# Linear attention and four-expert mixture: another opening, with other load queues, own buffers for each head pair and seven PSUM banks in the first layer

## The chip, the core and the metric

The kernel runs on one core of a Trainium2 chip. Its engines each take their instructions in order: PE multiplies matrices (its results go to PSUM, eight banks of 128 x 512 float32), DVE and ACT work element by element, POOL and SP here do little but issue DMA transfers. The metric is the device time of one execution in microseconds (us), less being better. Times in the profile count from the start of its span.

## The reference, cut to what matters

```python
q_p, k_p = phi(q), phi(k)             # phi(x) = where(x > 0, x, exp(x) - 1) + 1
kv  = einsum('bhsd,bhse->bhde', k_p, v)
z   = sum(k_p, axis=2)
num = einsum('bhsd,bhde->bhse', q_p, kv)
den = einsum('bhsd,bhd->bhs', q_p, z)[..., None] + 1e-06
x   = (num / den) as [4608, 512]      # 8 batches, 8 heads, 576 rows, 64 columns
p   = domain_probs / (domain_probs.sum(-1) + 1e-09)
for e in range(4):
    h = maximum(x @ w1[e], 0)         # w1[e]: 512 x 1024
    out += p[:, e:e+1] * (h @ w2[e])  # w2[e]: 1024 x 512
```

All inputs are float32; the kernel computes in float16 with float32 sums.

## The kernel before

The 576 rows of a batch are 512 rows, four of them on each of 128 partitions, and 64 rest rows. The 8 heads are taken as four pairs (`pr` 0 to 3). For each batch and pair, `attention` (L434) does: exp on ACT and two DVE operations for phi of k and of q (L456, L457), transposes of phi(q) (L484) and a copy to `qT` (L497), the sum kv with its column of ones for z (L515 to L523), a copy to `kvz` (L534), the numerator and denominator (L548, L550), and a division on DVE (L555, L556).

The mixture takes 512 rows at a time. Rows of batch 0 go through it in the plain way, an expert at a time: `first_l1` (L705) multiplies by w1 in chunks of 128 input columns (`dc`, four of them) and 128 hidden columns (`fj`, eight of them) and applies ReLU; `first_l2` (L744) multiplies by w2. All later rows go through units (`l1_seven`, `ssums`, `l2_unit`), which do each product in seven block products in place of eight, with sums of weight blocks that `sums_w1` and `sums_w2` prepare on DVE. Between the opening and the units, the attention of batch 1 runs among the mixture of experts 1 to 3 on batch 0.

The order is not that of the code. Every piece of work is handed to a `Plan` (L21) with an engine, an estimated duration, a priority and the keys that it reads and writes. The plan lays all pieces out in time, works deadlines back from PE, lays them out again, and the instructions are then written in that order, engine by engine. DMA pieces of POOL keep the order of the code. `T0` and `TU` (L163) are the planned start and pitch of the units. On the chip only the order and the waits on data count, not the planned times; the waits follow whole tiles, so that two users of different columns of one PSUM bank wait for each other.

Around the change:

- Loads (L293, L312): batch 0's pair 0 and its k and v rest rows are five DMAs in SP's queue; pairs 1 to 3 follow in POOL's, held until k of pair 0 has landed, and behind them the weights: w1 and w2 of expert 0, the q rest rows, expert 1, then batch 1's loads and experts 2 and 3. POOL has eight DMAs in flight at most. Weights and some of v turn to float16 on the way in.
- Buffers of batch 0's attention: three staging buffers for k, q and v, two `ek` and two `kqp`, used in turn; one PSUM bank each for transposes of phi(q) (`l2b[1]`), for the numerators (`at`) and for transposes of x (`tbank`, which is `l2b[3]`); kv and denominators share `l2b[2]`.
- Rest rows of k and v lie on 64 partitions (`kqr`, `vr`), a row of each head in a piece of 256 bytes.
- `turn_x` (L666) transposes the normalized rows of a pair into `xt0`, the right operand of the first layer; chunk `dc` of the first layer needs pair `dc`.
- `first_l1` for expert 0 runs four hidden chunks at once over `dc`, in four PSUM banks (`l1b` and `l2b[0]`), and the other four after them, three banks in turn. All ReLUs are ACT's (L713).
- `keep_warm` (L1073) fills planned gaps of PE up to 22 us (`WARM`) with matmuls whose result nobody reads.

Of the kernel before, what the change touches and what calls it, by code (L numbers as in the profile page):

```python
# [20 lines left out]
class Plan:  # L21
# [13 lines left out]
    def __init__(self):  # L35
        self.ops = []
        self.wr = {}
        self.rd = {}

    def add(self, eng, dur, pri, fn, r=(), w=(), move=0.0, after=0.0, lead=1.2):  # L40
        n = len(self.ops)
        deps = set()
        for key in r:
            if key in self.wr:
                deps.add(self.wr[key])
            self.rd.setdefault(key, []).append(n)
        for key in w:
            if key in self.wr:
                deps.add(self.wr[key])
            deps.update(x for x in self.rd.get(key, ()) if x != n)  # L50
        for key in w:
            self.wr[key] = n
            self.rd[key] = []
        self.ops.append(
            dict(eng=eng, dur=dur, pri=pri, fn=fn, deps=deps, move=move, after=after, lead=lead, w=w)
        )
        return n

    def deadlines(self):
# [10 lines left out]
        for n, o in enumerate(ops):  # L70
            if o["eng"] != "PE" and o["pri"] >= -99:
# [62 lines left out]
def kernel(  # L134
# [27 lines left out]
    WARM, COLD = 22.0, 28  # L162
    T0, TU = 79.0, 6.4  # L163
# [7 lines left out]
    def sb(name, shape, dt):  # L171
# [47 lines left out]
    v00 = vss[1].rearrange("p h c d -> p (h c d)").bitcast(FP16)[:, 2 * C * D :].rearrange(  # L219
        "p (h c d) -> p h c d", h=2, c=C  # L220
    )
    ones = sb("ones", [P, 2, 1], FP16)
    rc4 = sb("rc4", [P, 2 * C], FP32)
# [20 lines left out]
    def lk(i):  # L244

        return ("l2b2k", "l2b2n") if i == 2 else ("l2b%d" % i,)

    def stage_keys(i):

        if i < 2:  # L250
            return ("st", i, 0), ("st", i, 1), ("st", i, 2)
        return ("xp", 0), ("xp", 1), ("u2", 0)
# [35 lines left out]
    def v16(i):  # L288

        flat = vss[i].rearrange("p h c d -> p (h c d)").bitcast(FP16)  # L290
        return flat[:, 0 : 2 * C * D].rearrange("p (h c d) -> p h c d", h=2, c=C)

    def load_pair(b, pr, queue, pri, after=0.0, hold=None):  # L293
        hs = slice(2 * pr, 2 * pr + 2)
        n = 3 if b < 2 else 2
        i = rot("stage%d" % n, n) if n == 2 else rot("stage3", 3)
        stage[b, pr] = i
        kk = stage_keys(i)
        vo = vss[i] if b or queue == "SP" else v16(i)
        parts = [(k, kqs[i][:, 0], kk[0]), (v, vo, kk[2]), (q, kqs[i][:, 1], kk[1])]  # L300
        if b == 0:
            parts[1:] = parts[:0:-1]
        for t, o, key in parts:
            if (b, pr, key) == (0, 0, kk[1]):
                load_rest(0, "SP", 0, parts=(0,))
            keys = (key, "v00") if (b, key) == (1, ("st", 1, 2)) else (key,)
            dma(queue, pri, o, t[b, hs, 0:NT].rearrange("h (p c) d -> p h c d", c=C), keys,
                0.7,
                hold="w" if b == 2 else hold if key == kk[0] else None,
                mark="k0" if (b, pr, key) == (0, 0, kk[0]) else None, after=after)  # L310

    def load_rest(b, queue, pri, after=0.0, parts=(0, 1, 2)):  # L312
        par = b % 2
        rs = slice(par * R, par * R + R)
        for i in parts:
            t, o = ((k, kqr[rs, 0]), (v, vr[rs]), (q, kqr[rs, 1]))[i]
            dma(queue, pri, o, t[b, :, NT:S].rearrange("h s d -> s h d"), (("str", par, i),),
                1.1,
                hold="w" if b in (2, 3) else None, after=after)
# [26 lines left out]
    def probs(b0, b1, raw, keys, out_key, pri):  # L346
# [7 lines left out]
            r=keys, w=(out_key,))  # L354
# [10 lines left out]
    def rest_maps(b, pe_mode, pri, parts=(0, 1)):  # L365
# [19 lines left out]
        if not pe_mode:  # L385
            pl.add("SP", 1.25, pri + 1, lambda: nc.sync.dma_start_transpose(
                out=qTr[par][:, :, rs], in_=kqpr[rs, 1].rearrange("p h d -> p (h d)")),
                r=("qpr",), w=[("qTr", par, i) for i in range(DC)], move=0.9, lead=0.2)

# [44 lines left out]
    def attention(b, pr, pe_mode, pri, step, two=False):  # L434
# [16 lines left out]
        zi = pr if two else rot("kvz", 2)  # L451
# [8 lines left out]
        if two:  # L460
            vh = v00 if pr == 0 else v16(si)
            vk = "v00" if pr == 0 else sk[2]

        def vcast():
            if two:
                nc.scalar.copy(vh, vs)
            else:
                nc.scalar.copy(vp[:, :, :, 0:D].rearrange("p c h d -> p h c d"), vs)

        order_ = (0, 1)  # L470
        for i in order_:
# [4 lines left out]
            if i == 0 and not (two and pr):  # L476
                pl.add("ACT", 0.52, pri + step, vcast, r=(sk[2],), w=(vk,))
        if pe_mode:

            tq, tk = (l2b[1].bitcast(FP16), "l2b1") if two else (tbank, "l2b3")  # L480

            def turn():
# [4 lines left out]
                if two:  # L487
                    return
# [7 lines left out]
                   r=(("kqp", pi, 1), "ident") + (() if two else ("qpr",)), w=(tk,))  # L496
            pl.add("ACT", 0.5, pri + 3.5 * step, lambda: nc.scalar.copy(  # L497
                qT.rearrange("p c t -> p (c t)"), tq[:, 0:NT]), r=(tk,), w=(("qT", ti),))
            if not two:
                pl.add("DVE", 0.2, pri + 3.5 * step, lambda: nc.vector.tensor_copy(  # L500
                    qTr[par][:, pr, rs], tq[:, NT : NT + R]), r=(tk,), w=(("qTr", par, pr),))
# [6 lines left out]
        if two:  # L508
            kvs_, kvk = l2b[2][:, 0 : 2 * DE], ("l2b2k",)
        kv3 = kvs_.rearrange("p (h e) -> p h e", h=2)  # L510

        def kv():
            for c in range(C):
                if two:
                    nc.tensor.matmul(out=kv3[:, :, 0:D], lhsT=kp[:, c], rhs=vh[:, :, c],  # L515
                                     start=(c == 0), stop=False, skip_group_check=True)
                    nc.tensor.matmul(out=kv3[:, :, D:DE], lhsT=kp[:, c], rhs=ones,
                                     start=False, stop=False, skip_group_check=True)
                else:
                    nc.tensor.matmul(  # L520
                        out=kvs_, lhsT=kp[:, c], rhs=vp[:, c], start=(c == 0), stop=False
                    )
# [6 lines left out]
                skip_group_check=two,  # L529
# [7 lines left out]
        pl.add("PE", 0.42 if two else 0.3, pri + 4 * step, kv,  # L537
# [4 lines left out]

        if two:
            den = l2b[2][:, 256 : 256 + 2 * C].rearrange("p (c h) -> p c h", h=2)

            def nd0():
                for c in range(C):
                    nc.tensor.matmul(out=at[:, c * P : (c + 1) * P], lhsT=qT[:, c],  # L548
                                     rhs=kvz[:, :, 0:D], start=True, stop=True)
                    nc.tensor.matmul(out=den[:, c], lhsT=qT[:, c],  # L550
                                     rhs=kvz[:, :, D:DE], start=True, stop=True)

            def norm0():
                rc = rc4.rearrange("p (c h) -> p c h", h=2)
                nc.vector.reciprocal(rc, den)  # L555
                nc.vector.tensor_tensor(  # L556
                    out=xs[:, :, fs].rearrange("p c (h d) -> p c h d", h=2),
                    in0=at.rearrange("p (c h d) -> p c h d", c=C, h=2),
                    in1=rc[:, :, :, None].broadcast_to([P, C, 2, D]),
                    op=AO.mult,  # L560
                )

            pl.add("PE", 0.36, pri + 5 * step, nd0, r=(("qT", ti), ("kvz", zi)),
                   w=("at", "l2b2n"))
            pl.add("DVE", 0.83, pri + 5.5 * step, norm0, r=("at", "l2b2n"),
                   w=[("x", par, pr, c) for c in range(C)])
            return
# [77 lines left out]
    def sums_w2(e, pri):  # L645
# [11 lines left out]
        for o, a, b_, r, w in (  # L657
# [5 lines left out]
            pl.add("DVE", 0.62, pri, two(o, a, b_), r=r, w=w)  # L663


    def turn_x(pr, pri):  # L666
        fs = slice(pr * P, (pr + 1) * P)

        def go():
            for c in range(C):  # L670
                nc.tensor.transpose(
                    out=tbank[:, c * P : (c + 1) * P], in_=x_b[0][:, c, fs], identity=identh
                )

        pl.add("PE", 0.25, pri, go, r=[("x", 0, pr, c) for c in range(C)] + ["ident"], w=("l2b3",))
        pl.add("ACT", 0.5, pri + 0.5, lambda: nc.scalar.copy(xt0[:, pr, :], tbank[:, 0:NT]),
               r=("l2b3",), w=(("s4", 1, pr),))

    def mm1(e, fj, bank, dcs):
        for dc in dcs:  # L680
            nc.tensor.matmul(  # L681
                out=bank,
                lhsT=w1_sb[e][:, dc, fj * P : (fj + 1) * P],
                rhs=xt0[:, dc, :],
                start=(dc == 0),
                stop=(dc == DC - 1),
# [18 lines left out]
    def first_l1(e, pri, step, nb):  # L705
        ht = []
        banks = [(l1b[i], "l1b%d" % i) for i in range(3)]
        if nb == 4:
            banks += [(l2b[0], "l2b0")]
        ht = [rot("ht", len(hts)) for _ in range(FC)]  # L710

        def relu(fj, bank, key, pr_):
            pl.add("ACT", 0.5, pr_, lambda: nc.scalar.activation(hts[ht[fj]], bank, AF.Relu),  # L713
# [3 lines left out]
        if nb:  # L717
            b0 = cnt.get("l1", 0) if nb < 4 else 0
            for dc in range(DC):
                for fj in range(nb):  # L720
                    bank, key = banks[(b0 + fj) % nb]
                    p_ = pri + (dc * 4 + fj) * step
                    pl.add("PE", 0.216, p_,
                           lambda fj=fj, bank=bank, dc=dc: mm1(e, fj, bank, (dc,)),
                           r=w1k(e, dc, fj) + (("s4", 1, dc),), w=(key,))
                    if dc == DC - 1:
                        relu(fj, bank, key, p_ + 0.2)
            done = nb
            if nb == 4:
# [282 lines left out]
    load_pair(0, 0, "SP", 0)  # L1012
    load_rest(0, "SP", 0, parts=(1,))
    load_pair(0, 1, "POOL", 0, hold="k0")
    load_pair(0, 2, "POOL", 0)
    rest_maps(0, True, 3, (0,))
    for pr in range(DC):
        if pr == 3:
            load_pair(0, 3, "POOL", 0)
            load_w1(0, range(DC))  # L1020
            probs(0, 2, p5_b, ("p5",), "pnat0", 24)
            load_w2(0)
            load_rest(0, "POOL", 0, parts=(2,))
        attention(0, pr, True, 2.5 + pr, 0.4, two=True)
# [113 lines left out]
```

## Time and profile before

| | us |
|---|---|
| median of 7 runs | 498.86 |
| lowest and highest of the 7 | 497.93, 499.63 |
| profiled execution | 499.56 |
| span of its profile | 497.8 |
| PE busy in the span | 486.4 |
| DVE busy | 408.7 |
| ACT busy | 367.0 |

The span runs from the first to the last instruction of the program; the execution has 1.8 us more around it. Busy time of PE counts its filler matmuls too, and its ends are modelled, so it says where PE has instructions rather than how well it is used. In timelines a row is the start, the duration, the engine, the line, the operation and its tiles, how often it came in a row, and in brackets how long the engine had stood idle before it and what ended that. The name `w` covers w1 and w2, `s` covers the identity and some hidden tiles, `xp`, `u` and `vs` the staging buffers.

### The profile page before, as it was taken

How to read it: one execution, taken by the hardware profiler on the slowest of the kernel's cores; microseconds unless marked ns; L12 is line 12 of the kernel's file. 1: busy time of each engine (PE TensorE's matmuls, PEld its weight loads, DVE VectorE, ACT ScalarE, POOL GpSimd, SP SyncE). 2: the span in 40 equal slices, each digit the busy share in tenths (PEclk: the TensorE clock that was granted, in tenths of full speed). 3: DMA queues.
4: the chain of work that ended last, by engine and by line, in shares of the span. 5: the costliest groups of instructions: out<-in, count | busy, mean ns of one | idle time of the engine just before them, and what ended most of it. 6: DMA issues, size and time to landing. Idle time of an engine off the chain costs nothing.

```text
span 497.8 us, 15010 instructions
## 1 busy us (share of the span) xinstructions
PE 486.4 (98%) x6109; PEld 431.0 (87%) x6109; DVE 408.7 (82%) x1033; ACT 367.0 (74%) x690; POOL 41.7 (8%) x67
## 2 busy tenths in 40 slices
PE   7899999999999999999999999999999999999995
PEld 6544456999999999999999999999999999999995
DVE  5677999988998999899988899889988675767664
ACT  6635759988987798769876988689766767676641
POOL 7655710000000000000000000000000000000000
PEclk9999999999999999999999999999999999999999
DMA  8999988846674774765756765755623333523221
GB/s 227 197 235 196 262 169 187 222 103 175 126 161 121 167 170 133 128 167 118 171 126 158 148 150 119 169 139 123 161 54 85 36 97 43 77 55 86 45 44 42
DMA packets 125573, 67.11 MB, mean 135 GB/s; under 512 B 95520, under 2 KB 119600, under 8 KB 125504
## 3 DMA queue, kind: packets, MB, share of 16 engines
q1 hardware_dynamic: 116112, 51.79, 47.4%
q0 software_dynamic: 9232, 14.10, 14.0%
q8 instruction: 47, 0.77, 0.7%
q10 hardware_dynamic: 160, 0.26, 0.1%
q14 instruction: 22, 0.18, 0.1%
HBM read 45.16 MB, written 9.44 MB: 110 GB/s over the span
## 4 chain that ended last, share of the span: by engine, by line
PE 87%; DMA 7%; ACT 2%; DVE 1%; POOL 1%; issue 0%; DVEq 0%; POOLq 0%
PE l1b L835 40%; PE l2b L911 38%; DMA w<-in_moe_w_dram 4%; PE l2b L691 4%; PE l1b L681 3%; DMA kqr<-in_k_dram 2%; PE at L571 2%; DMA kq<-in_k_dram 2%; PE at L520 1%; ACT xp L795 0%; DVE ot L975 0%; POOL w L262 0%; ACT h L849 0%; ACT ek L379 0%; PE at L523 0%
## 5 line engine op out<-in xcount | busy, mean ns | idle before, releaser
L835 PEld LDWEIGHTS <-w 128*128 128x128 f16 x2048 | 133.4, 98 | 5.2
L849 ACT ACTIVATE h<-l1b 128x512 f16<-128x512 f32 x128 | 76.8, 600 | 53.6 <-PE l1b L835 48.4
L911 PE MATMUL l2b<-w,h 128*128 128x256 f16 x768 | 114.9, 273 | 0.0
L911 PE MATMUL l2b<-t,s 128*128 128x256 f16 x768 | 114.3, 273 | 0.0
L835 PEld LDWEIGHTS <-w1x 128*128 128x128 f16 x1536 | 100.1, 98 | 3.9 <-issue 0.2
L911 PEld LDWEIGHTS <-s 128*128 128x128 f16 x1024 | 90.9, 98 | 6.6
L855 DVE CUSTOM_DVE_ANT_0 h<-l1b,p 128x512 f16<-128x512 f32 x64 | 44.1, 690 | 46.0 <-PE l1b L835 42.7
L795 ACT ACTIVATE xp<-x,p_nat 128x512 f16<-128x512 f16 x112 | 77.5, 720 | 1.0 <-DVE x L584 0.5
L835 PE MATMUL l1b<-xT,w 128*128 128x128 f16 x1024 | 78.1, 219 | 0.0
L835 PE MATMUL l1b<-xs,w 128*128 128x128 f16 x1024 | 78.0, 219 | 0.0
L835 PE MATMUL l1b<-xs,w1x 128*128 128x128 f16 x1024 | 77.9, 219 | 0.1
L911 PEld LDWEIGHTS <-h 128*128 128x128 f16 x768 | 67.4, 98 | 4.5
L897 DVE TENSOR_TENSOR s<-h 128x512 f16<-128x512 f16 x128 | 53.9, 421 | 2.1
L852 ACT COPY l1b<-l1b 128x512 f32<-128x512 f32 x64 | 36.7, 574 | 12.2 <-PE l1b L835 11.5
L852 ACT COPY u<-l1b 128x512 f32<-128x512 f32 x64 | 37.5, 585 | 11.1 <-PE l1b L835 10.9
L855 DVE CUSTOM_DVE_ANT_0 h<-l1b,u 128x512 f16<-128x512 f32 x64 | 43.8, 685 | 1.1 <-PE l1b L835 0.4
L852 ACT COPY p<-l1b 128x512 f32<-128x512 f32 x64 | 37.4, 584 | 8.9 <-PE l1b L835 7.2
L472 ACT ACTIVATE ek<-kq 128x512 f16<-128x512 f32 x60 | 37.9, 632 | 4.8 <-DMA kq<-in_k_dram 3.9
L813 DVE TENSOR_TENSOR xs<-xT,xs 128x256 f16<-128x256 f16 x128 | 36.8, 288 | 3.4
L835 PE MATMUL l1b<-xT,w1x 128*128 128x128 f16 x512 | 39.0, 219 | 0.0
L911 PE MATMUL l2b<-w,s 128*128 128x256 f16 x256 | 38.4, 273 | 0.0
L457 DVE TENSOR_TENSOR kqp<-ek,kqp 128x512 f16<-128x512 f16 x64 | 27.2, 425 | 6.0 <-ACT ek L472 1.4
(128 smaller groups left out, 579.4 us busy)
## 6 DMA issues: line engine op xcount, KB each, us to landing
w<-in_moe_w_dram POOLq DMA_DIRECT2D x32, 256.0 KB, 8.3
out_dram<-ot SPq DMA_DIRECT2D x16, 512.0 KB, 3.6
kq<-in_k_dram SPq DMA_DIRECT2D x25, 256.0 KB, 3.2
kq<-in_q_dram SPq DMA_DIRECT2D x25, 256.0 KB, 3.6
vs<-in_v_dram SPq DMA_DIRECT2D x25, 256.0 KB, 3.7
kq<-in_k_dram POOLq DMA_DIRECT2D x5, 256.0 KB, 7.1
kq<-in_q_dram POOLq DMA_DIRECT2D x5, 256.0 KB, 6.1
xT<-xp SPq DMA_TRANSPOSE x64, 3.1
```

The costliest lines, as they stand in the source:

```text
L457: nc.vector.tensor_tensor(out=o, in0=ek[:, i], in1=o, op=AO.min)
L472: pl.add("ACT", 0.55, pri + i * step, lambda i=i: nc.scalar.activation(ek[:, i], kq[:, i], AF.Exp), r=(sk[i],), w=(("ek", ei, i),))
L681: nc.tensor.matmul(out=bank, lhsT=w1_sb[e][:, dc, fj * P : (fj + 1) * P], rhs=xt0[:, dc, :], start=(dc == 0), stop=(dc == DC - 1),)
L691: nc.tensor.matmul(out=bank, lhsT=hts[ht[fj]][:, c * P : (c + 1) * P], rhs=w2_sb[e][:, fj, :], start=(fj == 0), stop=(fj == FC - 1),)
L795: pl.add("ACT", 0.6, pri, lambda c=c, src=src, ps=ps: nc.scalar.activation(xp[:, c, :], src, AF.Copy, scale=ps), r=r, w=(("xp", xi, c),))
L813: lambda o=o, a=a, b_=b_: tt(out=o, in0=a, in1=b_, op=AO.subtract),
L835: nc.tensor.matmul(out=bank[:, fc * P : (fc + 1) * P], lhsT=wt[:, kc, fc * P : (fc + 1) * P], rhs=r[:, kc, :], start=(start and fc == 0 an ...
L849: return lambda: nc.scalar.activation(o, bank, AF.Relu)
L852: return lambda: nc.scalar.copy(o, bank)
L855: return lambda: nc.vector._custom_dve(TENSOR_ADD_SAT, out=o, in0=bank, in1=t, s0=BIG, s1=0.0)
L897: pl.add("DVE", 0.36, U(n + 1) + d - 0.5, lambda i=i, a=a, b_=b_, alu=alu: tt(out=s4[:, i], in0=a, in1=b_, op=alu), r=r, w=(Q(i),))
L911: nc.tensor.matmul(out=l2b[bank][:, half * HD : (half + 1) * HD], lhsT=a[:, c, :], rhs=w[:, c], start=(opens and first and c == 0), stop=( ...
```

## The change

The loads of batch 0 are issued one by one by `load_first` and `load_first_rest`. SP's queue has k and q of pair 0, k rest in two halves, k of pair 1, v rest in two halves and q of pair 1, eight DMAs. POOL has v of pair 0, k and q of pair 2, v of pair 1, w1 chunk 0 of expert 0, k and q of pair 3, v of pairs 2 and 3, and then the other weights in the order of before. For batch 1, w1 of expert 3 is loaded whole ahead of pair 3, and staging buffers are used in the order 0, 1, 2, 0.

Rest rows of k and v lie two to a partition on all 128 partitions, so that a piece is 512 bytes; their sum takes two matmul pairs for each head pair in place of one matmul. Each pair has its own staging, `ek` and `kqp`; they lie in tiles that the weight sums of experts 2 and 3 fill later, and `Plan.alias` carries that order. Every v is turned to float16 by its DMA. Transposes of phi(q) go to the two halves of `l2b[3]` and numerators to `at` and `l2b[1]` in turn; kv, denominators and the transposes of x share `l2b[2]`. The last pair is done in two halves from phi(q) on. The first layer of expert 0 sums seven hidden chunks at once in seven banks, its last `dc` in two column halves, and ReLUs of chunks 0, 2, 4 and 6 are DVE's. `WARM` is 13, `T0` is 77, and weight sums may start at 22 us.

```diff
-    WARM, COLD = 22.0, 28
-    T0, TU = 79.0, 6.4
+    WARM, COLD = 13.0, 28
+    LATE, RELU = 0.5, (0, 2, 4, 6)
+    T0, TU = 77.0, 6.4
...
+    def load_first(queue, pri, t, pr, hold=None, mark=None):
+        if t is v:
+            o, key = v_o[pr], ("v_o", pr)
+        else:
+            o, key = kqs[pr][:, int(t is q)], stage_keys(pr)[int(t is q)]
+        dma(queue, pri, o, t[0, 2 * pr : 2 * pr + 2, 0:NT].rearrange("h (p c) d -> p h c d", c=C),
+            (key,), 0.72, hold=hold, mark=mark)
+
+    def load_first_rest(t, o, queue, pri, key):
+
+        src = t[0, :, NT:S].rearrange("(g h) (p t) d -> h g p (t d)", h=2, t=2)
+        for h in range(2):
+            dma(queue, pri, o[:, h].rearrange("p t d -> p (t d)"), src[h], ((key, h),), 0.3)
...
+    def first_attention(pr, pri, step):
+
+        kq, sk = kqs[pr], stage_keys(pr)
+        ek, kqp, vh, kvz, qT = ek_o[pr], kqp_o[pr], v_o[pr], kvs[pr], qT_b[pr % 2]
...
+        ni = pr % 2
+        num = (at, l2b[1])[ni]
+        tq = tbank[:, ni * NT : (ni + 1) * NT]
+        kv3 = l2b[2][:, 0 : 2 * DE].rearrange("p (h e) -> p h e", h=2)
+        d0 = 136 + ni * 2 * C
+        den = l2b[2][:, d0 : d0 + 2 * C].rearrange("p (c h) -> p c h", h=2)
+        xt = l2b[2].bitcast(FP16)[:, NT : 2 * NT]
...
+        def kv():
+            parts = [(kqp[:, 0, c], vh[:, :, c], ones) for c in range(C)]
+            parts += [(kp_r[g, t], v_r[g, :, t], ones[g]) for t in range(2)]
...
+        parts = 2 if pr == DC - 1 else 1
...
-        if nb == 4:
-            banks += [(l2b[0], "l2b0")]
+        if nb > 3:
+            banks += [(l2b[0], "l2b0"), (at, "at"), (l2b[3], "l2b3"), (l2b[1], "l2b1")]
...
+            if nb > 3 and fj in RELU:
+                pl.add("DVE", 0.62, pr_, lambda: nc.vector.tensor_scalar(
+                    hts[ht[fj]], bank, 0.0, None, AO.max), r=(key,), w=(HTK[ht[fj]],))
+                return
...
+    load_first("SP", -9, k, 0, mark="k0")
+    load_first("SP", -8, q, 0)
+    load_first_rest(k, k_r, "SP", -7, "k_r")
+    load_first("SP", -6, k, 1)
+    load_first_rest(v, v_r32, "SP", -5, "v_r32")
+    load_first("SP", -4, q, 1)
+    load_first("POOL", 0, v, 0, hold="k0")
+    for pr in (2, 3):
+        load_first("POOL", 0, k, pr)
+        load_first("POOL", 0, q, pr)
+        if pr == 2:
+            load_first("POOL", 0, v, 1)
+            load_w1(0, (0,))
+    load_first("POOL", 0, v, 2)
+    load_first("POOL", 0, v, 3)
+    first_rest()
     for pr in range(DC):
...
+        first_attention(pr, 2.5 + pr, 0.4)
+    load_w1(0, range(1, DC))
...
-    ht = first_l1(0, 17.5, 0.1, 4)
+    ht = first_l1(0, 17.5, 0.1, 7)
...
-    load_pair(1, 3, "POOL", 0)
     load_w1(3, (2, 3))
+    load_pair(1, 3, "POOL", 0)
...
-        nc.tensor.matmul(out=l2b[1][:, 256:512], lhsT=identh,
+        nc.tensor.matmul(out=l1b[2][:, 256:512], lhsT=identh,
```

## The prediction, made before the changed kernel had run

> **What bounds the kernel now.** I read the busy lines, then busy time by stretches of 5 us, then the timelines of PE, DVE, ACT and POOL up to the first unit of the main loop.
>
> ```profile
> span 497.8 us, 15010 instructions
> PE 486.4 (98%) x6109; PEld 431.0 (87%) x6109; DVE 408.7 (82%) x1033; ACT 367.0 (74%) x690; POOL 41.7 (8%) x67
> ```
> PE is busy 98% of the span, so only a stretch where PE lacks real work can give time back. By stretches (columns: us, then PE, PEld, DVE, ACT, POOL busy, clock, DMA share, GB/s):
> ```profile
> 2.50:5.00 2.50, 2.45 (x12) 1.76 (x12) 2.01 (x10) 0.63 (x1) 1.10 (x2) 1.00 0.90 249
> 5.00:7.50 2.50, 2.50 (x14) 1.75 (x13) 1.37 (x4) 1.40 (x3) 2.50 (x4) 1.00 0.86 245
> 7.50:10.00 2.50, 2.27 (x25) 1.85 (x24) 1.43 (x4) 2.17 (x5) 2.50 (x5) 1.00 1.06 291
> 10.00:12.50 2.50, 2.44 (x35) 2.27 (x35) 0.51 (x2) 2.11 (x6) 2.50 (x5) 1.00 1.14 309
> 12.50:15.00 2.50, 1.28 (x21) 1.10 (x19) 2.18 (x6) 1.77 (x5) 2.50 (x5) 1.00 1.08 157
> ```
> DMA is full from 7.5 us on, and not quite before. The real start of PE is in its timeline (start, duration, line):
> ```profile
> 23.99 3.62 PE L681 MATMUL l1b<-s,w 128*128 128x512 f16 x16
> 27.45 5.34 PE L691 MATMUL l2b<-w,h 128*128 128x512 f16 x24
> 32.63 1.89 PE L681 MATMUL l1b<-s,w 128*128 128x512 f16 x8
> ...
> 41.79 1.02 PE L681 MATMUL l1b<-s,w 128*128 128x512 f16 x4 [0.68 <-ACT h L713]
> 42.65 0.59 PE L691 MATMUL l2b<-w,s 128*128 128x512 f16 x2
> ...
> 47.13 0.20 PE L489 MATMUL l2b<-s,kqpr 64*128 64x64 f16 x1 [0.27 <-DVE kqpr L375]
> ```
> From 23.99 us PE runs matmul after matmul (16 of 128x512 in 3.46 us to the next start: 0.216 us each) to the end, but for 0.68 and 0.27 us. Both waits come from ACT and DVE work on the second batch's loads:
> ```profile
> 41.88 0.63 ACT L472 ACTIVATE ek<-kq 128x512 f16<-128x512 f32 x1
> 42.42 0.58 ACT L713 ACTIVATE h<-l1b 128x512 f16<-128x512 f32 x1
> 43.30 0.63 ACT L379 ACTIVATE ek<-kqr 64x512 f16<-64x512 f32 x1 [0.30 <-DMA kqr<-in_k_dram]
> 43.95 1.08 ACT L713 ACTIVATE h<-l1b 128x512 f16<-128x512 f32 x2
> 45.06 0.62 ACT L382 CAST vpr<-vr 64x512 f16<-64x512 f32 x1
> 45.58 0.62 ACT L379 ACTIVATE ek<-kqr 64x512 f16<-64x512 f32 x1
> ```
> ReLUs of expert 1 stand in ACT's order behind exps that wait for q (landed 41.80) and k rest (43.27). The opening is therefore worth what PE gains by 24 us, as far as these loads let it through.
>
> [...] loads issued by POOL land 0.7 us apart [...]. [...] The rest rows are 256 B pieces now and 512 B after; k rest (128 KB) took 4.2 us to land, k of pair 0 (256 KB, 0.5 us earlier in the same queue) 2.9. [...] Here ACT's copy of kv waits 0.7 us for DVE's reciprocal, which reads other columns of l2b2. [...] Here the first filler matmuls follow each other at 0.213 us until 8.05 us, then at 0.109.
>
> **The change, part by part.**
>
> *Loads.* The same bytes. SP now carries k0, q0, k rest, k1, v rest, q1; POOL eight pair loads instead of nine, with w1 chunk 0 among them. At the 300 GB/s of 7.5 to 12.5 us, the stretches 2.5:5 and 5:7.5 leave (51+55) x 2.5 = 265 KB, or 0.9 us, unused: POOL's first loads arrive only 4.6 us after their issue at 3.9, and SP's have 256 B pieces. The new order fills both holes. Bounds: 0 (the holes stay), and 1.5 us: the first w1 chunk landed at 17.1 (10.55+6.6), 2.6 us after the last v, where later chunks take 1.25, so its early issue may hide part of that. I take 0.9 us, for all that lands later, since POOL keeps eight loads in flight and is held by landings (its waits on w: 8.6 us).
>
> *Attention of batch 0.* Own buffers and two tq and num banks take the false order between pairs away. Before, normalizations start at 12.58, 15.66, 18.75 and 20.76. By durations (exp 0.63, half of phi 0.43, PSUM copy 0.59, reciprocal 0.21, multiply 0.69, a hop 0.05 to 0.1): q0 lands at 4.35 and its phi ends at 5.8; the 24 fillers at 0.213 end at 7.7, turn(0) follows; v0 lands at 8.2 (3.9+4.5, now through POOL), kv 8.65, the copy waits behind exp of q1 (q1 lands at 8.0) until 9.6, ten fillers, nd to 10.3: norm(0) at 10.4, 2.2 earlier. Each later pair still queues in l2b2: kv copy after the earlier reciprocal, x turn after the kv copy, den after the x copy. That makes 2.9 us to norm(1) at 13.3 and 4.0 to norm(2) at 17.35, since PE's first dc group (0.86) and kv(3) stand before it. The last pair's halves follow at 19.8 and 20.4, and the last xt copy ends at 21.75 (22.83 before: 1.1 us). w1 chunks 1 to 3, which now block PE in order, land at 17.5, 18.8 and 20.0 (18.4, 19.7, 20.9 less 0.9): covered, but only by 0.2 us for chunk 1; a late one is late on the path. Bounds of this part: 0.7 earlier, 1.1 later.
>
> *Seven banks.* Before, 20 of 32 matmuls come after xt(3): 22.91 to 27.45. Now seven groups have gone ahead, and from 21.35 there are 19 matmul equivalents: 4.1 us, end at 25.45 instead of 27.45: **2.0 us**. Four ReLUs (0.62) go to DVE, idle there (2.93 of 5 us busy in 20:25), while PE has the fourth bank's work: no cost; without that cover 0.6.
>
> *L2 of expert 0* takes all four banks at once: 32 x 0.216 = 6.9 us, to 32.4; before, 24 and then 8 at 36.41. Same work, earlier order. w2 (last 26.3) and w1 of expert 1 (last 32.35, less 0.9 = 31.5) are there. L1 of expert 1 and the late rest rows (6.9+0.45) end at 39.8 instead of 42.65.
>
> *The wait that takes its place.* ACT's order now has exp k(1,0) before ReLU 5 and exp q(1,0) before ReLUs 6 and 7. q lands at 41.8-0.9 = 40.9: exp to 41.55, ReLU 6, ReLU 7 to 42.6. PE would want ReLU 7 at 39.8+10 x 0.216 = 41.95, so it waits 0.65. Then six matmuls to 43.95. kv(1,0) needs the v rest cast (43.35 to 43.95) and the v cast behind it (44.5): kv 44.55 to 44.85; four matmuls to 45.7, turn(1,0) to 46.05. Before, the turn ended at 47.33 with four matmuls (0.86) fewer done: 47.33+0.86-46.05 = **2.1 us** left. With a load gain of 0 the same steps give 47.1 and 1.1 us; with 1.5, 45.45 and 2.7.
>
> *Further on.* w1 of expert 2 (49.30-0.9 against L1 at 51.0-2.1, its last chunk wanted 0.65 later), w2 (56.35 against 58.84) and the last k and q pair, now behind all of w1 of expert 3 (1.5 us later, 1 us of slack at its turn), stay covered. DVE is idle 1.7 us between 47.10 and the first xs at 79.34; its chain starts 1.2 us earlier, xs come at 78.2, the first unit (81.77 before) wants them at 80.1. [...] The main loop has the same instructions in a slightly different order; I put it at 0, between -0.5 and +0.5 us by its near-zero PE waits.
>
> Sum: 2.1, less 0.1 for hops: 2.0 us off the span: 495.8. The profiled execution is 1.8 us longer than its span (499.56): 497.6. The median of the seven runs lies 0.7 below that execution, so **496.9 us**.
>
> **The rivals.** *Loads no earlier* (17%): DMA share is near 1 in the trace, which speaks for it; the two holes against. Gain 1.1: 497.8, down to 0.3. *More than foreseen* (7%): loads 1.5 us or more ahead: 496.1; for it, the 2.6 us at the first w1 chunk; against, that it shows before steady state alone. *Clock* (6%): fillers end at 13 us, PE drops to half speed in thin work; 5.5 us at half speed lose 2.7, L1 ends at 28.2, but later waits then vanish: gain 1.0 or less, 497.9. Against: PE works every 2 us there. *Slower* (10%): the plan starts the loop 2 us earlier (T0), so DMA transposes, loads and kv matmuls stand tighter in SP's and PE's order; PE then waits for xT or the kv operands at each of seven batches. At 0.5 us each, 3.5-2.0 = 1.5 us slower: 500.4; it decides from 0.43 us each (3.0 in all against 2.0, for a loss of 1.0). For it, DVE at 4.8 of 5 us around 80; against, xT lands 3 us ahead now (78.4 against 81.77).
>
> **How the numbers follow.** 60% for the forecast, whose own range is 496.1 to 497.8. 0.2% is 1.0 us, about what a measurement can tell. Faster: 60+7 and a few of the clock and load cases, 70%; same: the rest of these, 18%; slower: 12%, the loop with a little for an unseen wait. Range 495.9 to 498.9: it takes in the load cases and leaves out the slower one and half of the large gain.
>
> **What would show it.** First L1 group of expert 0 ended near 25.5 and L2's 32 matmuls in one piece after it; q(1,0) landing near 40.9; a PE wait on ACT of about 0.6 in L2 of expert 1; first unit near 79.7. Wrong if w1 chunks hold PE beyond 21 us, if q(1,0) lands at 41.8 or later, or if PE shows waits after 85 us.

## The result, and the profile after

The changed kernel takes **502.69 us** (median of 12 runs, 499.80 to 505.92), where the kernel before takes 498.71 (30 runs, 497.93 to 500.29): a ratio of **1.0085**, 95% interval 1.0068 to 1.0103. It is 0.85% slower; 0.4% faster was forecast. Its runs also scatter over 6 us, where those before stay within 2.4.

The profiled execution took 501.55 us. Its page, ahead of the groups:

```profile
span 499.4 us, 14992 instructions
PE 486.2 (97%) x6096; PEld 430.0 (86%) x6096; DVE 411.3 (82%) x1041; ACT 364.6 (73%) x687; POOL 41.4 (8%) x66
```

PE is busy as long as before (486.2 against 486.4 us) in a span that is 1.6 us longer, so PE is idle 1.8 us longer, and the place to look is again the start. The same stretches as in the prediction (us, then PE, PEld, DVE, ACT, POOL busy, TensorE clock, DMA share, GB/s):

```profile
2.50:5.00 2.50, 2.45 (x12) 1.72 (x12) 2.19 (x11) 1.25 (x2) 1.10 (x2) 1.00 0.84 236
5.00:7.50 2.50, 2.50 (x16) 1.77 (x14) 0.99 (x4) 0.43 (x2) 2.50 (x5) 1.00 1.02 218
7.50:10.00 2.50, 0.75 (x13) 0.59 (x11) 0.95 (x3) 0.63 (x1) 2.50 (x4) 1.00 0.98 274
10.00:12.50 2.50, 1.92 (x12) 1.38 (x12) 0.14 (x1) 1.03 (x3) 1.41 (x3) 0.61 1.17 275
12.50:15.00 2.50, 2.36 (x29) 1.77 (x27) 1.56 (x5) 2.44 (x6) 1.44 (x4) 0.71 1.24 251
```

Three things differ. From 5 to 7.5 us the DMA engines are full (1.02, before 0.86) but move fewer bytes (218 GB/s, before 245). From 7.5 to 10 PE works 0.75 us of 2.5 (before 2.27), and DVE works 0.14 us between 10 and 12.5. And the clock, 1.00 in every one of these rows before, is 0.61 and then 0.71. From 10.6 to 13.9 us alone it reads 0.50, from 14.1 to 17.4 again 1.00. So it was at half speed for 2 x 0.39 x 2.5 = 1.95 us of the one row and 1.45 us of the other, from about 10.55 to 13.95 us.

What the engines waited for stands in the waits up to 27 us (engine, line, releaser; us in total, times, longest):

```profile
DVE kqp L491 <- DMA kq<-in_q_dram: 3.7, 1, 3.7
ACT t L427 <- DMA w1x<-in_v_dram: 1.9, 1, 1.9
PE l2b L505 <- DMA w1x<-in_v_dram: 1.4, 1, 1.4
```

The second and third are v rest, whose cast on ACT kv(0) needs, and v of pair 0, which starts kv(0). The first is q of pair 1, the eighth load in SP's queue: issued at 4.86 us, landed at 12.34. It holds up the first normalization by way of ACT. There the exp of q of pair 1 stands ahead of the two copies of kv(0) to `kvz`, although kv(0) was complete by 11 us (its last matmul ran from 10.77 to 10.98). nd(0), the numerator and denominator of pair 0, needs these copies, and the normalization needs nd(0). ACT's timeline (start, duration, line):

```profile
12.36 0.63 ACT L548 ACTIVATE ek<-kq 128x512 f16<-128x512 f32 x1 [1.34 <-DMA kq<-in_q_dram]
12.90 0.19 ACT L509 CAST kvz<-l2b 64x65 f16<-64x65 f32 x1
13.11 0.21 ACT L510 CAST kvz<-l2b 64x65 f16<-64x65 f32 x1
```

DVE has mapped q of pair 1 (L491, L492) by 13.45 and then still waits 0.69 us for nd(0) before the reciprocal (L521) that opens each normalization:

```profile
12.36 0.45 DVE L491 TENSOR_SCALAR kqp<-kq 128x512 f16<-128x512 f32 x1 [3.70 <-DMA kq<-in_q_dram]
...
14.14 0.21 DVE L521 RECIPROCAL rc<-l2b 128x8 f32<-128x8 f32 x1 [0.69 <-PE l2b L516]
...
17.22 0.21 DVE L521 RECIPROCAL rc<-l2b 128x8 f32<-128x8 f32 x1 [0.49 <-ACT t L548]
...
21.44 0.21 DVE L521 RECIPROCAL rc<-l2b 128x8 f32<-128x8 f32 x1 [1.29 <-PE l2b L505]
...
24.00 0.18 DVE L521 RECIPROCAL rc<-l2b 128x4 f32<-128x4 f32 x1 [1.63 <-PE l2b L516]
```

Before, they came at 12.58, 15.66, 18.75 and 20.76. PE's timeline has the thin stretch, the slow fillers, nd(0) (L514) and what follows:

```profile
7.40 0.39 PE L496 MATMUL l2b<-s,kqp 128*128 128x128 f16 x4
9.22 0.22 PE L505 MATMUL l2b<-w1x,kqp 128*128 128x128 f16 x1 [1.44 <-DMA w1x<-in_v_dram]
...
10.91 2.31 PE L1170 MATMUL l1b<-qTr,s 128*128 128x256 f16 x10
13.36 0.26 PE L514 MATMUL at<-kvz,qT 128*128 128x128 f16 x1
...
29.75 7.07 PE L771 MATMUL l2b<-w,h 128*128 128x512 f16 x32
...
82.88 0.61 PE L922 MATMUL l1b<-xT,w 128*128 128x128 f16 x8
```

The ten fillers at 10.91 take 2.31 us, 0.23 each, where 14 in a row take 1.69 us in the kernel before (from 10.06, at a clock of 1.00): half speed. The first L1 of expert 0 ends at 29.75 (27.45 before, 25.45 forecast), and the first unit of the loop starts at 82.88 (81.77 before, 79.7 forecast). The later loads did come earlier: the last w1 chunk of expert 0 at 20.27 (20.89 before), q of pair (1,0) at 39.70 (41.80).

Two theories followed. **Late operands**: q of pair 1, and the v rest rows ahead of it, land late, and the opening with them. **Clock**: PE's thin stretch from 7.8 us lets the clock fall, by an amount that differs from run to run. The twelve runs of the changed kernel speak for the second: their granted clock lies between 0.981 and 0.999 and sorts them almost perfectly (499.80 us at 0.999; 501.00 and 501.55 at 0.996; 502.52 at 0.993; 505.43 and 505.92 at 0.981). A third came in as the runs went on, **the shared bank**: kv, denominators and x transposes of all pairs go through one bank (`l2b2`), which stretches the distance from pair to pair.

### The profile page after: what moved, and what is told of

The parts are those of the page before. It is cut to its first block, busy times and chain, and to the rows that moved or that the text cites. A ratio compares the mean times of both kernels' runs of the same rounds, so it can differ in the third digit from the quotient of the medians.

```text
span 499.4 us, 14992 instructions
## 1 busy us (share of the span) xinstructions
PE 486.2 (97%) x6096; PEld 430.0 (86%) x6096; DVE 411.3 (82%) x1041; ACT 364.6 (73%) x687; POOL 41.4 (8%) x66
## 4 chain that ended last, share of the span: by engine, by line
PE 92%; DMA 3%; ACT 1%; SPq 1%; DVE 1%; issue 1%; DVEq 0%; ACTq 0%
PE l1b L922 39%; PE l2b L998 39%; PE l2b L771 4%; PE l1b L760 4%; PE at L663 2%; DMA kq<-in_q_dram 1%; PE at L639 1%; SPq L292 1%; DMA kq<-in_k_dram 1%; DMA xT<-xp 1%; PE l2b L760 1%; DVE ot L1062 0%; PE l2b L505 0%; ACT s L570 0%; PE l2b L531 0%
## 5 line engine op out<-in xcount | busy, mean ns | idle before, releaser
L939 ACT COPY u<-l1b 128x512 f32<-128x512 f32 x64 | 37.5, 586 | 10.4 <-PE l1b L922 9.9
L604 ACT ACTIVATE ek<-kq 128x512 f16<-128x512 f32 x54 | 33.8, 629 | 0.7 <-DMA kq<-in_k_dram 0.6
L984 DVE TENSOR_TENSOR s<-s,h 128x512 f16<-128x512 f16 x64 | 27.1, 424 | 5.1
```

What stands on the lines that cost most here:

```text
L604: pl.add("ACT", 0.55, pri + i * step, lambda i=i: nc.scalar.activation(ek[:, i], kq[:, i], AF.Exp), r=(sk[i],), w=(("ek", ei, i),))
L939: return lambda: nc.scalar.copy(o, bank)
L984: pl.add("DVE", 0.36, U(n + 1) + d - 0.5, lambda i=i, a=a, b_=b_, alu=alu: tt(out=s4[:, i], in0=a, in1=b_, op=alu), r=r, w=(Q(i),))
```

## The experiments

All kernels but one are edits of the changed kernel. "norm" is the start of each pair's normalization (the first half of pair 3), "L1" the end of the first L1 of expert 0, "unit" the start of the loop's first unit; all in the one profiled execution of each. "x banks" stands for x transposes in the banks of the numerators. Medians are of all runs of a kernel, ratios are to the kernel before in runs on the same chip. Times of one execution scatter: before and before with WARM 13 have the same median, and their first units lie 0.8 us apart.

| kernel | norm 0, 1, 2, 3 | L1 | unit | clock in the runs | runs | median us | ratio (95%) |
|---|---|---|---|---|---|---|---|
| before | 12.58, 15.66, 18.75, 20.76 | 27.45 | 81.77 | 0.99 to 1.0 | 30 | 498.7 | 1 |
| changed | 14.14, 17.22, 21.44, 24.00 | 29.75 | 82.88 | 0.981 to 0.999 | 12 | 502.69 | 1.0085 (1.0068 to 1.0103) |
| before, WARM 13 | 12.57, 15.66, 18.24, 20.24 | 26.87 | 80.95 | 0.997 to 1.0 | 13 | 498.72 | 0.9996 (0.9987 to 1.0005) |
| fillers | 14.15, 17.27, 21.48, 24.05 | 29.79 | 82.92 | 0.997 to 1.0 | 5 | 501.20 | 1.0049 (1.0037 to 1.0061) |
| v rest on POOL | 13.09, 16.96, 22.30, 25.29 | 31.26 | 84.39 | 0.987 to 0.996 | 6 | 501.69 | 1.0066 (1.0050 to 1.0081) |
| the same with fillers | 13.38, 16.45, 20.67, 23.75 | 29.64 | 82.76 | 0.996 to 0.999 | 6 | 501.10 | 1.0048 (1.0036 to 1.0060) |
| q1 and v rest on ACT | 13.57, 16.67, 20.89, 23.46 | 29.20 | 82.33 | 0.981 to 0.999 | 8 | 500.62 | 1.0054 (1.0030 to 1.0078) |
| v rest on ACT | 13.24, 16.76, 20.98, 23.54 | 29.29 | 82.41 | 0.986 to 0.997 | 6 | 501.29 | 1.0058 (1.0038 to 1.0078) |
| v rest on ACT, 18 fillers | 12.10, 15.18, 19.40, 21.96 | 27.70 | 80.83 | 0.996 to 1.0 | 22 | 499.41 | 1.0015 (1.0007 to 1.0022) |
| fillers, x banks | 14.16, 16.75, 20.14, 21.95 | 27.91 | 81.23 | 0.994 to 1.0 | 13 | 499.47 | 1.0016 (1.0006 to 1.0026) |
| v rest on ACT, 8 fillers, norm(2) first | 13.35, 17.22, 21.71, 26.16 | 33.14 | 86.28 | 0.984 to 1.0 | 22 | 499.21 | 1.0020 (1.0006 to 1.0033) |
| v rest on ACT, 8 fillers, x banks | 12.20, 14.71, 18.11, 19.92 | 25.88 | 79.21 | 0.997 to 1.0 | 11 | **497.80** | 0.9980 (0.9971 to 0.9988) |
| that with T0 79 | 12.15, 14.66, 18.05, 19.86 | 25.81 | 79.14 | 0.997 to 1.0 | 9 | 497.88 | 0.9981 (0.9972 to 0.9990) |
| that (T0 77) with four banks | 12.66, 15.16, 18.84, 20.65 | 27.43 | 80.47 | 0.997 to 1.0 | 13 | 498.75 | 0.9995 (0.9987 to 1.0003) |

**Fillers.** After the plan is laid out, more filler matmuls go ahead of the second and third of PE's steps, kv(0) and nd(0):

```diff
+    EXTRA = {1: 20, 2: 12}
...
                     keep_warm()
+                for _ in range(EXTRA.get(npe, 0)):
+                    keep_warm()
+                npe += 1
                 free = o["start"] + o["dur"]
```

> The changed kernel with 20 more filler matmuls between the first query transpose and kv(0), and 12 more between kv(0) and nd(0). The theory of the clock (PE is nearly idle from 7.8 to 10.9 us, the clock falls to half for one or more windows, and how many of them decides the time of a run) expects no half-speed record in the trace, a granted clock of 0.999 in every run, all runs within 1.5 us of each other, and a median of 499.5 to 500.3, where the changed kernel has 502.7 and 499.8 to 505.9. The theory of the loads (q of pair 1 lands at 12.3 us and holds up DVE, the clock matters little) expects 502 to 503 as before; both expect q of pair 1 still at about 12.3 and the first L1 of expert 0 to end no earlier than 29.

The clock in this trace is full (same columns as above):

```profile
7.50:10.00 2.50, 2.50 (x28) 2.26 (x27) 1.30 (x4) 0.84 (x2) 2.23 (x5) 1.00 1.03 265
10.00:12.50 2.50, 2.08 (x27) 1.85 (x26) 0.00 (x0) 0.89 (x2) 1.49 (x3) 1.00 1.14 257
```

In five runs the 6 us of scatter shrink to 0.43 (500.83 to 501.26) and the median falls by 1.5 us. DVE still does nothing from 10 to 12.5, q of pair 1 lands at 12.55, and norm and L1 stay where they were to 0.05 us. So the clock is the scatter and 1.5 us of the median, about half of what was expected of it; the rest, 2.5 us against the kernel before, has another cause. In the one execution of the changed kernel that was profiled, the fall of the clock cost nothing up to L1: its slow fillers end at about 13.2 us, and nd(0) had to wait for the copies until 13.32. The loss is in the runs with a lower clock, such as the one profiled with norm(2) first (0.984), where L1 ends at 33.14.

**The kernel before with WARM 13.**

```diff
-    WARM, COLD = 22.0, 28
+    WARM, COLD = 13.0, 28
```

> The kernel before with fillers planned up to 13 us only instead of 22, the part of the change that takes fillers away later on. If the missing fillers after 13 us let the clock fall, it shows half-speed records and 500 to 503 us with a spread; if the fall comes from the thin stretch at 7.8 to 10.9 us of the changed kernel, which the kernel before doesn't have, it stays at 498.7 with a clock of 0.999.

Nothing: 498.72, with a full clock in its trace. In the kernel before it is harmless that fillers end at 13 us. In the changed kernel's trace the clock fell for what comes earlier: PE's first gap has 24 fillers instead of 34, and PE then waits 1.44 us for v ahead of kv(0). That fillers end at 13 us is not cleared for every edit of it, though: in three of the traces below the clock falls again or for the first time between 20.7 and 22.5 us, where the kernel before still had fillers.

**v rest through POOL**, alone and with fillers. Moves are made after the plan, so that all other orders stay:

```diff
+    MOVES = [(("v_r32", 0), "POOL", ("v_o", 0)), (("v_r32", 1), "POOL", ("v_r32", 0))]
...
         todo = pl.order()
+        for key, queue, behind in MOVES:
+            o = todo.pop(find(key))
+            o["q"][0] = queue
+            todo.insert(find(behind) + 1 if behind else 0, o)
```

> The changed kernel with the two v rest loads issued by POOL behind v of pair 0 instead of by SP ahead of q of pair 1; the order on all other engines is kept. The theory of the loads expects q of pair 1 to be issued at 3.9 and to land by 10 us, DVE's wait for it to fall from 3.7 us to about 1, the first normalization to come at 12 instead of 14.14, the first L1 of expert 0 to end near 27.7 instead of 29.75, and a median about 2 us lower (500.7), with the spread from the clock still there. The theory of the clock alone expects at most 0.5 us from it, since PE's thin stretch from 7.8 to 9.2 stays. If loads of one queue only change places, v rest lands later and kv(0) takes over the wait: then no gain.

> Both edits: v rest through POOL, and fillers, 12 before kv(0) and 6 before nd(0). If the late load and the clock are two causes that add up, the clock is 0.999 in every run, the first L1 of expert 0 ends near 27.5, and the median is 497 to 498, below the kernel before (498.7). If the clock is the one cause, it is as with the fillers alone (about 500). If the load alone, it is as with the load alone.

q of pair 1 lands at 8.78 and 8.51, as expected, and DVE no longer waits 3.7 us for it. But now v rest lands at 10.38 and 10.27, its cast on ACT stands ahead of the copies and of the exp of q, and norm(0) comes at 13.1 to 13.4 instead of 12. In the first trace the clock is at half speed from 12.23 to 19.06 (0.50 in the rows from 12.5 to 17.5) and from 22.47 to 25.88 (0.50 from 22.5 to 25), and L1 ends later than without the edit; in the second, from 20.77 to 24.18 (0.65 and 0.67 in the two rows from 20 to 25). The third possibility named, that v rest takes over the wait, is most of the answer. The edit with fillers (EXTRA 12 and 6) also shows what fillers can cost: 16 of them, from 11.03 on, hold nd(0) until 12.79, though the copies of kv(0) were done at 12.09.

**q of pair 1 and v rest on ACT; v rest alone on ACT.** Both ahead of ACT's table load; the second kernel lacks the entry of `("st", 1, 1)`, which is q of pair 1, and SP keeps that load:

```diff
-    MOVES = [(("v_r32", 0), "POOL", ("v_o", 0)), (("v_r32", 1), "POOL", ("v_r32", 0))]
+    MOVES = [(("v_r32", 1), "ACT", None), (("v_r32", 0), "ACT", None), (("st", 1, 1), "ACT", None)]
```

> The changed kernel with q of pair 1 and both v rest loads issued by ACT as its first instructions, ahead of its table load; all other orders kept. Theory of the late operands (kv(0) and norm(0) wait for whichever of q of pair 1 and v rest comes last, because SP's later loads share the 16 engines with POOL's): all three land by 8.5 us, norm(0) starts at 10.7 to 11.3 instead of 14.14, and the later normalizations follow at the same spacing (3.1, 4.2, 3.1 us), so that the first L1 of expert 0 ends near 26.5 instead of 29.75 and the median falls by 2 us or more to 499 to 500, less if the clock falls. Theory that the bytes set it (the first 1.5 MB take until 9 us in any order): k or q of pair 0 lands later by as much as q of pair 1 lands earlier, and norm(0) comes at 12.5 or later.

> The changed kernel with only the v rest loads moved to ACT, ahead of its table load; q of pair 1 goes out on SP as the seventh load (3.7 us). Late operands: v rest lands by 7, q of pair 1 at 8.5 to 8.8 as in the run with v rest on POOL, v of pair 0 at 9.0 is then last, kv(0) runs at 9.0, norm(0) at 10.7 to 11.3; first L1 of expert 0 ends near 26.5. Bytes: as above, norm(0) at 12.5 or later.

Neither reaches 11 us. With both on ACT, q of pair 1 lands at 4.54 and q of pair 0 at 5.29 instead of 4.36, k of pair 1 at 9.31 instead of 7.55, v of pair 0 at 9.83 instead of 9.18. With v rest alone on ACT, q of pair 1 lands at 9.92 and v of pair 0 at 10.22. The loads change places, as the theory of the bytes has it. Both traces also have a half-speed stretch over norm(0), and here it does cost time: the ten planned fillers, begun at 10.63 and 10.91, take 2.31 and 1.71 us (1.26 in the run with 18 fillers, where the clock reads 1.00) and hold nd(0) until 12.74 and 12.41, where the copies were done at 11.59 and 11.45. So the comparison with the clock kept up was still missing:

> v rest issued by ACT and 18 fillers ahead of kv(0), nothing else: the loads alone with the clock kept up. Against fillers alone: norm(0) at 12.3 to 12.6 instead of 14.15, the same spacings of 3.1 to 3.5, 4.2 and 2.6, L1 to end near 28.2 instead of 29.79, median 499.7 to 500.2 instead of 501.2. If norm(0) stays at 13 or later, what the run of the same loads without these fillers showed (13.24, at half clock) was not the clock but ACT's order.

With 18 fillers ahead of kv(0) (EXTRA 18, none further on) norm(0) is at 12.10, the spacings are 3.08, 4.22 and 2.56, and L1 ends at 27.70: 2.05 and 2.09 us earlier than with fillers alone, the median 1.8 us lower. Late operands are thus worth about 1.8 us. The kernel with fillers alone has 12 more ahead of nd(0), and a part of the 1.8 us may be theirs. In its trace they end just when the copies of kv(0) do (13.52, nd(0) at 13.57), and norm(0) is as late in the changed kernel, which has none of them; but where q of pair 1 lands earlier they can hold nd(0), as a trace further on shows. But norm(0) at 12.10 is still 1.7 us from the 10.4 of the prediction: v of pair 0 lands at 9.68 here, and at 9.18 in the changed kernel.

**x transposes in the numerators' banks**, with the fillers of the first run. A numerator is dead once its normalization has read it:

```diff
-        xt = l2b[2].bitcast(FP16)[:, NT : 2 * NT]
+        xt, xk = l2b[2].bitcast(FP16)[:, NT : 2 * NT], "l2b2x"
+        if pr < DC - 1:
+            xt, xk = num.bitcast(FP16)[:, 0:NT], ("num", ni)
...
-                w=("l2b2x",))
+                w=(xk,))
...
-                xt0[:, pr, ts], xt[:, ts]), r=("l2b2x",), w=(("s4", 1, pr),))
+                xt0[:, pr, ts], xt[:, ts]), r=(xk,), w=(("s4", 1, pr),))
```

> The changed kernel with the fillers of the first run (20 ahead of kv(0), 12 ahead of nd(0)) and the x transposes of pairs 0 to 2 in the bank of their own numerator; the loads as in the changed kernel. Against the run with these fillers alone (norm at 14.15, 17.27, 21.48, 24.05; first L1 of expert 0 ended at 29.79; 501.2): the theory that the shared bank stretches the pairs expects norm(0) unchanged at 14.1 and spacings of 2.5, 3.4 and 1.8 us as in the run that has both edits, L1 to end at 27.8 and the median at about 499.2. If the spacing shrank there because of the earlier loads, the spacings stay at 3.1, 4.2 and 2.6 and the time at 501.

DVE's timeline of this run, the reciprocals again:

```profile
14.16 0.21 DVE L524 RECIPROCAL rc<-l2b 128x8 f32<-128x8 f32 x1 [1.18 <-PE l2b L519]
16.75 0.20 DVE L524 RECIPROCAL rc<-l2b 128x8 f32<-128x8 f32 x1
20.14 0.21 DVE L524 RECIPROCAL rc<-l2b 128x8 f32<-128x8 f32 x1 [0.48 <-PE l2b L508]
21.95 0.18 DVE L524 RECIPROCAL rc<-l2b 128x4 f32<-128x4 f32 x1 [0.87 <-PE l2b L519]
```

norm(0) is unmoved (here the 22 fillers hold nd(0), until 13.57 where the copies were done at 12.84), the spacings are 2.59, 3.39 and 1.81 instead of 3.12, 4.21 and 2.57, and the waits in the brackets are shorter or gone. L1 ends 1.88 us earlier and the median falls by 1.7. The shared bank is a cause of its own, as large as the late loads. Of the 1.7 us, 1.3 are in the span and 0.4 in the time outside it (2.2 us with fillers alone, 1.8 here).

**Both, and the order of norm(2).** Both have v rest on ACT. The first has 8 fillers ahead of kv(0) and the normalization of pair 2 put before kv(3) (`todo.insert(kv3, todo.pop(n2))`); the second the same fillers and the x banks:

> As the run before (v rest on ACT) with 8 fillers ahead of kv(0), and with the normalization of pair 2 put ahead of kv(3) in the order, so that its reciprocal doesn't wait for kv(3) in the bank that they share. If the spacing of 4.2 us between norm(1) and norm(2) is that wait, it falls to about 3.5; kv(3) then waits about 0.3 longer. With the load theory right: the first L1 of expert 0 ends near 26, clock 0.997 or more in every run, median 498.3 to 499. With neither right: 501, as with fillers alone.

> v rest on ACT, 8 fillers ahead of kv(0), and the x transposes of pairs 0 to 2 written into the bank of their own numerator, which is dead by then, instead of into the bank that holds kv and the denominators (the plan is laid out anew, so the loop's order may differ by a few tenths). If the shared bank sets the spacing of the pairs, norm(1), norm(2) and norm(3) follow each other 0.5 us closer each, and the first L1 of expert 0 ends near 25.5; median 497.5 to 498.5. If ACT's and DVE's order sets it, nothing changes against the run without it.

The first says nothing on the order. In its profiled execution the clock was at half speed from 12.15 to 18.95 and again from 22.4 to 29.2. These are two of its stretches; the two between them read 0.50:

```profile
10.00:12.50 2.50, 1.91 (x22) 1.61 (x22) 1.23 (x4) 2.43 (x7) 1.52 (x3) 0.93 1.12 272
17.50:20.00 2.50, 2.50 (x21) 1.28 (x20) 2.26 (x7) 0.63 (x2) 1.62 (x3) 0.71 1.15 199
```

Its median is 0.2 us under that of 18 fillers without the new order, and that may be the fillers. Eight fillers did not keep its clock up in all 22 runs. The second has the lowest median of all kernels tried. Its page and PE's timeline:

```profile
span 495.7 us, 15022 instructions
...
25.88 7.07 PE L777 MATMUL l2b<-w,h 128*128 128x512 f16 x32
79.21 0.61 PE L928 MATMUL l1b<-xT,w 128*128 128x128 f16 x8
```

Against fillers alone it gains 3.4 us, where loads and bank apart gained 1.8 and 1.7: they add up. It is 0.2% faster than the kernel before.

**T0, and four banks**, both from that version:

```diff
-    T0, TU = 77.0, 6.4
+    T0, TU = 79.0, 6.4
```

```diff
-    ht = first_l1(0, 17.5, 0.1, 7)
+    ht = first_l1(0, 17.5, 0.1, 4)
```

> The best version so far (v rest on ACT, 8 fillers, x transposes in the numerators' banks) with T0 back at 79 instead of 77. That version needs 416.5 us from its first unit to the end, the kernel before 415.95 to 416.0. If the earlier T0 costs the loop this half microsecond, the loop goes back to 416.0 and the median to 497.3; if the loop's order is a matter of chance, 497.5 to 498.5. The opening up to the first unit keeps its times in both.

> The best version so far with four banks in the first L1 instead of seven. The prediction counted 19 matmul equivalents after the last x transpose with seven banks and 20 matmuls plus the wait with four: the first L1 of expert 0 should end about 0.9 us later (26.8 instead of 25.9), and the median rise by 0.5 to 0.9 us, to 498.3 to 498.7. If w1 or ACT's ReLUs decide there, no difference.

T0 does nothing that shows: 497.88 against 497.80, and 416.6 us from the first unit to the end, where that version has 416.5 and the kernel before 416.0. With four banks L1 ends 1.55 us later, of which 0.73 is there already when the last x copy ends: in that execution v of pair 0 landed 0.45 us later. The rest of L1's delay is the banks. ACT's last x copy, and the L2 that follows L1, with four banks:

```profile
22.47 0.37 ACT L576 COPY s<-l2b 128x256 f16<-128x256 f16 x1 [0.36 <-PE l2b L537]
...
27.43 0.81 PE L777 MATMUL l2b<-w,h 128*128 128x512 f16 x3
```

That is 27.43 - 22.84 = 4.59 us from the end of the copy, and with seven 25.88 - 22.11 = 3.77. The medians differ by 0.95 us.

## Why the prediction was wrong, step by step

The landing times failed, and with them the start of the attention; the clock, held unlikely, took another 1.5 us. The parts on seven banks and on L2 came out as forecast.

**Loads.** The step that failed first, and that made norm(0) late. It took q of pair 1 to land at 8.0 and v of pair 0 at 8.2; they landed at 12.34 and 9.18. It priced the new order by filling two holes at 300 GB/s, and it put nothing down for what two queues at work do to each other. That POOL's loads land 0.7 us apart in the trace before tells nothing of it: SP's last load had landed there at 8.12, ahead of POOL's first at 8.52, and from 7.5 to 10 us the packets of POOL's queue took 105.4% of the time of the 16 DMA engines and those of SP's 0.4%. In the changed kernel, in the same stretch, it is 59.3% for POOL's queue and 38.6% for SP's. The first four loads of POOL land at 9.18, 10.82, 11.76 and 12.65 there. The holes in DMA share were filled, but not with bytes (218 GB/s at a share of 1.02), and SP's last load came in 7.5 us after its issue, beside POOL's, where its first two took 2.9 and 3.1. Mended (v rest on ACT), norm(0) still is no earlier than 12.10, because v of pair 0 lands at 9.68. From v's landing to norm(0) it is 2.4 us there, and 2.2 in the prediction: the chain was right (it had the copy of kv(0) behind the exp of q of pair 1), its first landing wrong by 1.5. That all later loads come earlier was right: 0.9 us was taken, 0.6 (w1 of expert 0) to 2.1 (q of pair (1,0)) was measured.

**Attention of batch 0.** 10.4 was forecast for norm(0), and 14.14 came; the spacings forecast (2.9, 4.05 and 2.45) were near those measured (3.08, 4.22 and 2.56). So the last x copy ended at 26.20 instead of 21.75, of which 3.74 is the start. The queueing in `l2b2` was in the forecast too, rightly sized; what it didn't ask is what this queue costs against the kernel before (3.08, 3.09, 2.01), where the x transposes had another bank. With the x banks it falls to 2.59, 3.39 and 1.81, and the kernel by 1.7 us.

**Seven banks.** Right. From the last x copy to the end of L1 3.7 us were forecast, and 3.55 and 3.77 measured, where four banks take 4.6. **L2 in one piece** and w1, w2 in time: right, 32 matmuls in 6.91 us from start to next start.

**The wait in its place.** It did not come: with q of pair (1,0) at 39.70, L2 of expert 1 shows no wait for ACT. From L1 to the first unit the kernel with fillers takes 1.1 us less than forecast, 0.65 of it this wait. In the best version turn(1,0) ends at 45.63 and the first unit starts at 79.21, where 46.05 and 79.7 were forecast: with its opening mended, the forecast for the first unit nearly holds, though by a different sum (norm(0) 1.8 later, spacings 1.7 shorter).

**Main loop.** 0, between -0.5 and +0.5, was forecast. The changed kernel's trace has +0.5 us (499.4 - 82.88 = 416.5 against 416.0), but with fillers alone, which leave the loop as it is, it is 416.1, and the eight traces with this loop lie between 416.1 and 417.3. So a loss in the loop isn't shown, and T0 makes no difference. The time outside the span did grow: it is 2.1 to 2.2 us in the changed kernel, with fillers and with loads on ACT (medians of their runs), a little under 2.0 with v rest on POOL, and 1.8 before and in every kernel with the x banks. Why is open.

**Rivals.** "Clock" had 6% and the right mechanism, but its place and its price were wrong: in the changed kernel's trace it is not the end of the fillers at 13 us (alone it does nothing to the kernel before) but the early gap, and it is not a gain cut to 1.0 but a loss of 1.5 at the median and of up to 5 in a run. The reason given against it, that PE works every 2 us there, was true and no protection: ahead of the fall PE was idle for 1.44 us at most. "Slower" had 10% for the main loop, which was to lose 3.5 us; no more than 0.5 is seen there, and that not in every trace.

The miss of 5.8 us, from 496.9 to 502.7, adds up as follows. The clock is 1.5. The other 4.3 can be read from the trace with fillers: the opening is 3.2 (82.92 against 79.7 at the first unit), the loop nothing (416.1, as in the forecast: 495.8 - 79.7), the time outside the span 0.4. The last 0.7 is what the forecast took off because the median before lay so far below its profiled execution; with fillers both are 501.20.

## What to carry to other kernels

Ask of each load in a reordered opening when it lands beside all others in flight, and which engine stands in order behind it; here the last load of one queue was late once a second queue ran (7.5 us from issue to landing, where the first two took 2.9 and 3.1), and moving it to a third moved part of the delay to other loads (v of pair 0 from 9.18 to 9.83). Count what a bank is used for before giving its neighbours away: a bank that serves several steps of every pair is a queue, and the banks won for L1 (0.95 us) were lost nearly twice over in it (1.7). When work at the start is rearranged, look at PE's busy share over every few microseconds, and at the clock of several runs: here the runs scattered with their clock (0.981 to 0.999) where PE had a thin stretch (1.10 us of work in 3.4), and some twenty more fillers ahead of kv(0) mended it (0.996 to 1.0). Count fillers against the real waits: with few the clock could fall (with eight, to 0.984 in the run profiled with norm(2) first, though the best version stayed at 0.997 or more with as many), and those that stand ahead of a step that is ready hold it up (nd(0) by 0.56 to 0.73 us in five traces).

## What the hardware did that was not expected

The clock fell though PE was never idle for more than 1.44 us at a time: between 7.15 and 10.55 us, the 3.4 us ahead of the fall, PE worked for 1.1 us in two pieces (to 7.79, and from 9.22 to 9.70). It stayed down for 3.4 us, and in the other trace shown for 6.8, twice that. Within one execution these times lie on a grid. The first fillers run at half pace (0.213 us each, in rows where the clock column reads 1.00), and the end of that start, the falls and the rises lie whole multiples of 3.41 us apart, to 0.05 us: 7.18, 10.56 and 13.98 in the changed kernel; 5.45, 12.23, 19.06, 22.47 and 25.88 with v rest on POOL; 5.27, 12.14, 18.96, 22.38 and 29.20 with norm(2) first. One step of this grid is a window here. From one of these three executions to the next the grid lies elsewhere. If it does so between runs of one kernel too, it cuts the same thin stretch differently each time. That would explain why 12 runs of the changed kernel had clocks from 0.981 to 0.999, but it was not shown: the grid of those runs, all but one, isn't on record.

The length of a single gap doesn't decide it: in the changed kernel the clock fell after gaps of 1.44 us at most, while the best version has a gap of 2.08 us ahead of kv(0), and no run of it is under 0.997. A share of busy time in the window doesn't decide it either. PE was busy for 1.10 of 3.41 us ahead of the changed kernel's fall, but with v rest on POOL a window with 1.53 passed (5.40 to 8.82) and one with 1.78 led to a fall (8.82 to 12.23); and a window with 2.50 (17.4 to 20.8) passed in the changed kernel and led to a fall with v rest on POOL and fillers. What decides a fall isn't settled here.

Over the twelve runs, time goes with the clock at about 0.34 us for each 0.001 of its mean ((505.92 - 499.80) / 18). By my estimate one window at half speed is 0.0034 of the mean clock (half of 3.41 in 499.4 us), so the slowest runs, at 0.981, had about five of them. The two profiled runs shown fit: one window at half speed with a clock of 0.996, four with 0.984.

DMA engines at a share of 1.02 moved 218 GB/s between 5 and 7.5 us, and at 0.86 they had moved 245 before. With fillers alone, the loads unmoved, the same stretch moved 223 GB/s at a share of 0.95; with v rest on POOL 256 at 1.01, and 245 at 0.96 with fillers beside it; with v rest on ACT and 18 fillers 248 at 1.00. What costs this is not separated.
